# Attention and a tanh-shrink MLP: another order for the first batch's second layer, with weight rounding and weight combinations moved along with it

## The chip, the core and the metric

The kernel runs on one core of a Trainium2 chip. The core has a matrix engine (TensorE, "PE" in the profile, with its weight loads as "PEld"), a vector engine (VectorE, DVE), an activation engine (ScalarE, ACT), a general engine (GpSimd, POOL), and a queue engine (SyncE, SP) that issues the transfers between device memory and the core. Each engine works through its own list of instructions in order; an instruction that has to wait holds up everything behind it on that engine. The metric is the device time in microseconds (us) of one execution.

## What is computed

Attention over 8 batches and 12 heads, whose result is the input of a two-layer MLP:

```python
# q, k, v: (8, 12, 448, 64);  w_in: (768, 2048);  w_out: (2048, 768)
q_n = q / sqrt(mean(q * q) + 1e-6) * g_q          # k_n in the same way
attn = softmax(q_n @ k_n.T / sqrt(64)) @ v
x = attn.transpose(0, 2, 1, 3).reshape(8 * 448, 768)
h = x @ w_in
out = (h - tanh(h)) @ w_out
```

The weights are given in float64 and are rounded to float32 on the chip.

## The kernel before

The work goes in 48 attention steps (a step s is one batch and a pair of heads; six steps make a batch). Beside the attention of later steps runs the MLP of earlier batches, as a stream of matmuls that is cut into slices: `run(ns)` takes matmuls from the stream `mlp()` until their nominal time is used up, so that the order of all engines is fixed when the program is written. The MLP's matmuls are saved by a Strassen-like scheme: seven products (`ORDER` = 1, 5, 6, 2, 3, 7, 4) in place of eight, for which sums and differences of weight blocks and of activations are needed.

The first batch is special, because its weights are still being made ready. Its first layer (`hidden(0)`) is 28 products (4 groups j of 7), beside the steps 6 to 9. Its second layer (`project_first`, L1309) is plain: 6 chunks of 128 output columns, each the sum of 16 matmuls over the rows f of `w_out`, with 448 columns moving; 96 matmuls m in all, beside the steps 9 to 12. The chunks come one after another, each in its own PSUM bank (`mm_bank()`, three in turn): first the chunks 3 to 5, whose weights are the right half of `w_out` (`w_half[1]`), then 0 to 2 (`w_half[0]`). After the 16th matmul of a chunk ScalarE copies the bank out (L1345), VectorE transposes it (L966), and `step_out` later issues four transfers to the output.

The weights come in 32 pieces of 128 x 768 values (`PIECES`), 16 of `w_in` and 16 of `w_out` (pieces 16 to 23 the right half, 24 to 31 the left half, each holding two rows f). A piece n goes through these stages:

- SP loads it into a buffer `w_raw` (L290, L294), 768 KB. There are three buffers, and the load of piece n + 3 waits until piece n has left its own.
- `round_weight_a` on ScalarE (L71, L72), which waits for the load.
- `round_weight_b` on VectorE (L78, L79, L82); it is issued when the next piece takes the first stage.
- `round_weight_c` on POOL (L92 twice), after which the buffer is free.

How far `weight(to)` goes is a plan: `due` (L815) for the 28 products of the first layer, which end with 24 pieces done, and in the second layer the piece count 24 + 8 (m + 1) / 48 for its first 48 matmuls. For pieces of `w_in`, `combine` adds four combinations per group on VectorE (L357), one each product. Blocks that later batches need are written back to device memory (`keep_step` L372, `keep_w_out` and `keep_factors` L388).

For the second layer of later batches, `combine_w_out(f)` (L375) makes four combinations of `w_out` rows f and f + 8 on VectorE (L381 to L384, 128 x 384 each) into two slots of the ring `w_f` (six slots), and leaves behind two transfers to device memory, which are issued one round later. Before, this is done for f = 0 to 7 at the matmuls m = 52, 56, ... 80. The ring is then loaded for the next batch (`ring_load(2)` at m = 84 and `ring_load(4)` at 86).

The attention of a step s in this region (`early_slot`, L1448) emits, on PE: the sums over the keys (`totals`, L700) into a bank of the score pool, whose reciprocal VectorE takes (L705); the scores of the next step (L569), whose exponentials ScalarE takes (L575); a slice of 8 MLP matmuls; the transposes of the step after (`turn`, L467 and L471), the first of which goes to the bank that the reciprocal has just read; another 8 matmuls; then the remaining scores (with `p_last` for the last keys), the values (L623, L677), and `divide` on VectorE (L777, xT). The score pool has five banks that are taken in turn. From step 11 on, `visit` (L647) does this work, and takes `totals` of steps 11 and 12 to a bank of the MLP's pool.

Of the kernel before, what the change touches and what calls it, by code (L numbers as in the profile page):

```python
# [147 lines left out]
def bounded_path(tc, ctx, q, k, v, moe_w_in, moe_w_out, out, g_col, ident, ones, half_ones, neg_half, early):  # L148
# [29 lines left out]
    EARLY, PIECES = 8, 2 * CF  # L178
    HS = S // 2
    HC, HF = CD // 2, CF // 2  # L180
    SETS = CF // 4
# [83 lines left out]
    def w_out_row(f, i):  # L265
        return w_half[i][f // 2][:, f % 2]
# [35 lines left out]
    def weight_dst(n):  # L302
        return weight_piece(n)[2].rearrange("p f n -> p (f n)")
# [17 lines left out]
    def weight(to):  # L321

        while done[1] < min(to, PIECES):
            n = done[1]
            keep_step(0, {CF - 4: 0, CF: 1, CF + HF: SETS - 1}.get(n, -1))
            round_weight_a(nc, raws[n], weight_dst(n))
            settle(n)
            done[1] = n + 1
            load_weights(n + (3 if n < EARLY - 3 else 4))
            if kept[1] < kept[0] and n >= 4 * kept[0] + 2:  # L330
                keep_weights()
            keep_step(2)
        if done[1] == PIECES:
            settle(PIECES)
# [40 lines left out]
    def combine_w_out(f):  # L375

        a11, a21 = (w_out_row(f, i) for i in range(2))
        a12, a22 = (w_out_row(f + HF, i) for i in range(2))
        t = [ring_slot() for _ in range(2)]
        s3, s1, s2, s4 = (t[i // 2][:, i % 2 * HALF : (i % 2 + 1) * HALF] for i in range(4))  # L380
        nc.vector.tensor_tensor(out=s1, in0=a21, in1=a22, op=ALU.add)  # L381
        nc.vector.tensor_tensor(out=s3, in0=a11, in1=a21, op=ALU.subtract)
        nc.vector.tensor_tensor(out=s2, in0=s1, in1=a11, op=ALU.subtract)
        nc.vector.tensor_tensor(out=s4, in0=a12, in1=s2, op=ALU.subtract)  # L384
        late["keep"].append(lambda: [keep_factors(3 + 2 * i, 2, f, t[i]) for i in range(2)])

# [165 lines left out]
    def sc_bank():  # L552
        return bank_of("sc")
# [93 lines left out]
    def visit(s, av):  # L647

        wave(*half_values(s, 2, av, True))
        for c in range(2):  # L650
            v0, v1 = half_values(s, c, av, False)
            if has(s + 1):
                (s0, exp0), (s1, exp1) = scores(s + 1, c, True)
                wave(s0, v1)
                exp0()
                wave(v0, s1)
                exp1()
            else:
                wave(v0, v1)
        last_values(s, av)  # L660
        del loaded["v", s]
        if s >= FOLDED:
            divide(s, av)
        if has(s + 1):
            scores(s + 1, 2)
        if s < FOLDED:
            totals(s, mm_bank())
            divide(s, av)

    def values(s, av, chunks=(2, 0, 1)):  # L670
# [14 lines left out]
    def totals(s, dn):  # L685

        parts = [t[:, h, n * HS : (n + 1) * HS] for t in sums.get(s, ()) for n in range(2) for h in range(2)]
        parts = [(parts, [ones[:, :BL]] * 2)] if parts else []
        if not sums.pop(s):
            for p in full(s):  # L690
                parts.append(
                    ([p[:, h, n * HS : (n + 1) * HS] for n in range(2) for h in range(2)], [ones[:, :BL]] * 2)
                )
            last = probs[s, KF]
            parts.append(([last[:, h, 0] for _ in range(2) for h in range(2)], [half_ones[:, n] for n in range(2)]))
        for i, (moving, by) in enumerate(parts):
            for n in range(2):
                for h in range(2):
                    r = (2 * n + h) * BL
                    nc.tensor.matmul(  # L700
                        dn[r : r + BL, :HS], lhsT=by[n], rhs=moving[2 * n + h],
                        start=(i == 0), stop=(i == len(parts) - 1),
                    )
        rs = whole[s] = sp.tile([P, HS], F32, name="rs")
        nc.vector.reciprocal(rs, dn[:, :HS])  # L705
# [106 lines left out]
    late = {}  # L812


    due = [EARLY + (CF - EARLY) * (m + 1) // (7 * SETS // 2) for m in range(7 * SETS // 2)]  # L815
    due += [CF + HF * (m + 1) // (7 * SETS // 2) for m in range(7 * SETS // 2)]
    assert len(due) == 7 * SETS and due[-1] == CF + HF

    def part(name):
        if name == "th" and "blocks" in late:  # L820
            late["turn"] = (late.get("turn", 0) + 1) % 3
            if late["turn"] == 0:
                return late["blocks"].tile([P, 2, HS], F32, name="th_more")
        return tp.tile([P, 2, HS], F32, name=name)
# [484 lines left out]
    def project_first(b):  # L1309

        g = late["g"]
        for fn in late["todo"]:
            fn()
        late["todo"] = []
        keep_step(0, SETS - 1)
        took = 4 * S / ENGINE_NS
        for m in range(CD * CF):
            k, f = m // CF, m % CF
            n = (k + HC) % CD
            if f == 0:  # L1320
                bank = mm_bank()
            if f == CF // 2:
                step_out(2)
            if k < HC:
                weight(CF + HF + HF * (m + 1) // (HC * CF))
            elif m < HC * CF + 2:
                keep_w_out(PIECES - 2 + m - HC * CF)
            elif (m - HC * CF) % 4 == 0 and m - HC * CF <= 4 * HF:
                for fn in late["keep"]:
                    fn()  # L1330
                late["keep"] = []
                combine_w_out((m - HC * CF) // 4 - 1)
            elif m == CD * CF - 12:
                ring_load(2)
                for fn in late["keep"]:
                    fn()
            elif m == CD * CF - 10:
                ring_load(4)
            nc.tensor.matmul(  # L1339
                bank[:, :S], lhsT=w_out_row(f, n // HC)[:, n % HC * P : (n % HC + 1) * P], rhs=g[:, f, :],  # L1340
                start=(f == 0), stop=(f == CF - 1),
            )
            if f == CF - 1:
                y = part("s2").rearrange("p f s -> p (f s)")
                nc.scalar.copy(out=y, in_=bank[:, :S])  # L1345
                store(b, n, y)
            yield took
        wp_stack.close()
        late["blocks"] = pool("blocks", bufs=1)
        late["second"] = pool("second", bufs=1)  # L1350
        late["tg"] = single_stack.enter_context(tc.tile_pool(name="tg", bufs=1))
        late["inner"] = inner_steps()
# [527 lines left out]
```

## Time and profile before

| | us |
|---|---|
| median of 3 runs (1344.12 to 1344.48) | 1344.18 |
| the profiled execution | 1342.53 |
| its span, first to last instruction | 1340.7 |
| PE busy in the span | 1311.5 (98%) |
| VectorE busy | 969.5 (72%) |
| POOL busy | 795.0 (59%) |
| ScalarE busy | 568.1 (42%) |
| granted TensorE clock, mean | 0.998 |

The page's chain of waits gives 83% of the span to PE, 7% to VectorE and 4% to POOL. The regions that the change touches are the first layer of the first batch, whose matmuls (L857 on `w_out` and `w_f` buffers) run from 76.6 to 175 us, and its second layer (L1339), from 176.3 to 268.5. A timeline line has start, length, engine, source line, operation, output and inputs, shape and count; the bracket at the end is the idle time of the engine just before and who ended it. "PE <-DVE rs L705" there means that PE stood idle until VectorE's instruction of line 705 was done.

### The profile page before, as it was taken

Reading aid. Unit: us, or ns where it says so; the run is one execution under the profiler, and the core shown is the slowest. Engines: PE = TensorE matmul, PEld = TensorE weight load, DVE = VectorE, ACT = ScalarE, POOL = GpSimd, SP = SyncE. Lnnn points to the kernel's source line nnn. Section 1 sums busy time; section 2 is a strip of 40 time slices with the busy share of each in tenths; the row PEclk is TensorE's granted clock in tenths of the full one; section 3 lists DMA queues with packets and bytes.
Section 4 is the critical chain, followed back from the end, with each engine's and each line's share of the span. In section 5 each row is a group of like instructions: output and inputs, shape, how many; then the busy total and the mean of one; then the engine's idle time right before and its main releaser. Section 6 shows DMA issues by size and latency. Waiting matters only on the chain.

```text
span 1340.7 us, 29301 instructions
## 1 busy us (share of the span) xinstructions
PE 1311.5 (98%) x11368; PEld 1033.4 (77%) x11368; DVE 969.5 (72%) x1410; ACT 568.1 (42%) x1328; POOL 795.0 (59%) x591
## 2 busy tenths in 40 slices
PE   7989999999999999999999999999999999999997
PEld 3467854488998888688878788779887888799986
DVE  4999978867765767688888576768888667634455
ACT  7856654244343454445322445454512254311102
POOL 4766776348846256726698245944699244812771
PEclk9999999999999999999999999999999999999999
DMA  7779889889999766476655867466745776466544
GB/s 169 183 214 262 265 260 231 250 278 279 340 284 287 181 160 180 112 186 155 171 149 136 201 162 183 117 170 165 181 132 145 150 201 161 118 161 172 170 142 102
DMA packets 364759, 253.53 MB, mean 189 GB/s; under 512 B 273028, under 2 KB 303300, under 8 KB 364612
## 3 DMA queue, kind: packets, MB, share of 16 engines
q1 hardware_dynamic: 364608, 251.57, 69.1%
q8 instruction: 92, 1.51, 0.5%
q14 instruction: 55, 0.45, 0.1%
q10 hardware_dynamic: 4, 0.00, 0.0%
HBM read 205.23 MB, written 46.27 MB: 188 GB/s over the span
## 4 chain that ended last, share of the span: by engine, by line
PE 83%; DVE 7%; POOL 4%; DMA 2%; SPq 2%; issue 2%; ACT 1%; DVEq 0%; ACTq 0%; POOLq 0%
PE mm L857 38%; PE mm L1142 21%; PE sc L569 9%; PE sc L635 6%; PE mm L1339 5%; POOL u L1099 3%; PE sc L623 1%; POOL rr_mine L523 1%; PE sc L677 1%; DVE w_out L357 1%; PE mm L677 1%; SPq L497 1%; DVE rs L705 1%; DMA w_f<-w_inner 1%; DVE w_out L82 0%
## 5 line engine op out<-in xcount | busy, mean ns | idle before, releaser
L857 PE MATMUL mm<-xT,w_f 128*128 128x224 f32 x1296 | 263.5, 353 | 0.8 <-DVE xT L767 0.8
L857 PEld LDWEIGHTS mm<-xT,w_f 128*128 128x128 f32 x1296 | 244.8, 190 | 5.5 <-issue 4.2
L569 PE MATMUL sc<-qT,kT 64*32 64x448 f32 (+1 forms) x3072 | 215.6, 499 | 2.7 <-ACT p_last L575 2.1
L857 PE MATMUL mm<-tt,w_f 128*128 128x224 f32 x1044 | 212.6, 355 | 0.2 <-DMA w_f<-w_in 0.2
L857 PEld LDWEIGHTS mm<-tt,w_f 128*128 128x128 f32 x1044 | 195.8, 190 | 15.9 <-issue 15.4
L523 POOL TENSOR_TENSOR rr_mine<-rr_mine,neg_half 128x28 f32<-128x28 f32 x33 | 162.2, 4915 | 2.7
L762 DVE TENSOR_TENSOR xT<-xT,sc 128x448 f32<-128x448 f32 x34 | 21.0, 618 | 165.8 <-PE sc L569 114.8
L1142 PE MATMUL mm<-u,w_f 128*128 128x224 f32 x672 | 137.2, 354 | 1.0 <-POOL u L1099 0.5
L905 POOL TENSOR_TENSOR gT<-s,th 128x448 f32<-128x448 f32 x44 | 57.8, 1313 | 132.2 <-ACT th L904 128.7
L1142 PE MATMUL mm<-gT,w_f 128*128 128x224 f32 (+3 forms) x512 | 132.0, 412 | 1.2 <-DVE acc L1149 0.9
L1142 PEld LDWEIGHTS mm<-u,w_f 128*128 128x128 f32 x672 | 126.1, 190 | 8.0 <-POOL u L1099 3.6
L569 PEld LDWEIGHTS sc<-qT,kT 64*32 64x32 f32 x3072 | 72.4, 106 | 68.1 <-issue 49.2
L1142 PEld LDWEIGHTS mm<-gT,w_f 128*128 128x128 f32 x512 | 93.9, 190 | 34.3 <-issue 32.0
L635 PE MATMUL sc<-p,v_nat 64*32 64x448 f32 x1184 | 116.9, 536 | 0.0
L1142 PE MATMUL mm<-g,w_f 128*128 128x224 f32 (+1 forms) x360 | 98.9, 428 | 0.0
L575 ACT ACTIVATE p<-sc 128x448 f32<-128x448 f32 x132 | 71.9, 545 | 50.3 <-PE sc L569 37.4
L905 POOL TENSOR_TENSOR g<-s,th 128x448 f32<-128x448 f32 x24 | 30.3, 1264 | 105.1 <-ACT th L904 105.1
L1142 PEld LDWEIGHTS mm<-g,w_f 128*128 128x128 f32 x360 | 67.9, 190 | 26.5 <-issue 26.0
L729 ACT COPY sum_g<-sum 32x14 f32<-32x14 f32 x280 | 56.3, 201 | 72.0 <-DVE sum L721 66.3
L1339 PE MATMUL mm<-gT,w_out 128*128 128x448 f32 x192 | 74.0, 542 | 0.0
L145 POOL TENSOR_TENSOR rr<-rr,neg_half 112x8 f32<-112x8 f32 (+1 forms) x30 | 49.8, 1689 | 35.5 <-DVE rr L144 35.0
L1099 POOL TENSOR_TENSOR u<-gT 128x448 f32<-128x448 f32 x48 | 63.5, 1342 | 11.1 <-PE mm L1142 11.1
(206 smaller groups left out, 2465.8 us busy)
## 6 DMA issues: line engine op xcount, KB each, us to landing
w_f<-w_in SPq DMA_DIRECT2D x196, 384.0 KB, 3.5
w_f<-w_inner SPq DMA_DIRECT2D x63, 512.0 KB, 3.7
w_f<-w_out SPq DMA_DIRECT2D x42, 512.0 KB, 3.9
w_raw<-in_moe_w_out_dram SPq DMA_DIRECT2D x16, 768.0 KB, 5.4
w_in<-w_out SPq DMA_DIRECT2D x21, 384.0 KB, 5.3
qk_nat<-in_q_dram SPq DMA_DIRECT2D x132, 56.0 KB, 2.6
qk_nat<-in_k_dram SPq DMA_DIRECT2D x132, 56.0 KB, 2.4
g<-w_out SPq DMA_DIRECT2D x14, 512.0 KB, 5.4
```

Of the source, the lines that this page charges most:

```text
L145: nc.gpsimd.tensor_tensor(out=r, in0=r, in1=neg_half[:rows], op=ALU.pow)
L523: nc.gpsimd.tensor_tensor(out=mine, in0=mine, in1=neg_half[:, :1].to_broadcast([P, 2 * NJ]), op=ALU.pow)
L569: nc.tensor.matmul(tiles[h][i * BL : (i + 1) * BL, :n], lhsT=kT[r, c * P + at : c * P + at + BL], rhs=qT[r, first : first + n], start=True ...
L575: nc.scalar.activation(p[:, h, c if c < 2 else 0, :], tiles[h][:, :n], AF.Exp, scale=1.0 if rr is None else rr[:, 0, 2 * c + h : 2 * c + h ...
L635: nc.tensor.matmul(av[g][i * BL : (i + 1) * BL, :S], lhsT=v_nat[keys, h, c, m * BL : (m + 1) * BL], rhs=p[keys, h], start=first, stop=True ...
L677: nc.tensor.matmul(av[n][r : r + BL, :HS], lhsT=v_nat[:, h, c, m * BL : (m + 1) * BL], rhs=p[c][:, h, n * HS : (n + 1) * HS], start=False, ...
L729: nc.scalar.copy(out=acc[h * BL : (h + 1) * BL, g], in_=part[g * BL : (g + 1) * BL, h * NJ : (h + 1) * NJ])
L857: nc.tensor.matmul(bank[:, f * HS : (f + 1) * HS], lhsT=w[:, c * width + f, :], rhs=moving[p](c), start=(first and f == 0 and c == 0), sto ...
L905: eng.tensor_tensor(out=g[:, rows, cols], in0=h, in1=th, op=ALU.subtract)
L1099: nc.gpsimd.tensor_tensor(out=u[:, half], in0=a[:, half], in1=z[:, half], op=ALU.subtract)
L1142: nc.tensor.matmul(bank[:, :n], lhsT=w(i), rhs=mv, start=(first and i == 0), stop=(i == len(moving) - 1), skip_group_check=not first,)
L1339: nc.tensor.matmul(bank[:, :S], lhsT=w_out_row(f, n // HC)[:, n % HC * P : (n % HC + 1) * P], rhs=g[:, f, :], start=(f == 0), stop=(f == C ...
```

## The change

The first layer takes 14 pieces in its 28 products and ends with 22 done, where it took 16 and ended with 24; its plan starts two products later. The second layer then takes ten pieces in its first 44 matmuls (`behind`). To have time for the last two pieces of the right half, it works on three chunks at once: for each row f the three matmuls of three chunks, in three banks, twice. The copies and stores of three chunks then come together, at m = 45 to 47 and 93 to 95, into three different buffers. The combinations of `w_out` come at m = 24, 30, 36, ... 66. For the last two rows the four combinations leave in four transfers and not two. The ring loads come at m = 80 and 84. As the three MLP banks are all in use, `visit` takes `totals` of the steps 11 and 12 to the score pool.

```diff
-        late["keep"].append(lambda: [keep_factors(3 + 2 * i, 2, f, t[i]) for i in range(2)])
+        if f < HF - 2:
+            late["keep"].append(lambda: [keep_factors(3 + 2 * i, 2, f, t[i]) for i in range(2)])
+            return
+        late["keep"].append(lambda: [keep_factors(3 + n, 1, f, s) for n, s in enumerate((s3, s1, s2, s4))])
...
         if s < FOLDED:
-            totals(s, mm_bank())
+            totals(s, sc_bank())
...
-    due = [EARLY + (CF - EARLY) * (m + 1) // (7 * SETS // 2) for m in range(7 * SETS // 2)]
-    due += [CF + HF * (m + 1) // (7 * SETS // 2) for m in range(7 * SETS // 2)]
+    SOON_OUT, LAST_OUT = HF - 2, 44
+    due = [EARLY + (CF - EARLY + SOON_OUT) * max(m - 1, 0) // (7 * SETS - 2) for m in range(7 * SETS)]
+    behind = [min(PIECES, CF + SOON_OUT + (PIECES - CF - SOON_OUT) * (m + 1) // LAST_OUT) for m in range(CD * CF)]
...
         for m in range(CD * CF):
-            k, f = m // CF, m % CF
-            n = (k + HC) % CD
-            if f == 0:
-                bank = mm_bank()
-            if f == CF // 2:
-                step_out(2)
-            if k < HC:
-                weight(CF + HF + HF * (m + 1) // (HC * CF))
-            elif m < HC * CF + 2:
-                keep_w_out(PIECES - 2 + m - HC * CF)
-            elif (m - HC * CF) % 4 == 0 and m - HC * CF <= 4 * HF:
+            k, f, i = m // (HC * CF), m % (HC * CF) // HC, m % HC
+            n = (1 - k) * HC + i
+            if m % 4 == 3:
+                step_out()
+            weight(behind[m])
+            if f == 0:
+                bank = [] if i == 0 else bank
+                bank.append(mm_bank())
+            if LAST_OUT <= m < LAST_OUT + 2:
+                keep_w_out(PIECES - 2 + m - LAST_OUT)
+            if m >= CF + HF:
+                keep_combined((m - CF - HF) // 6 + 1)
...
-            elif m == CD * CF - 12:
+            if m == CD * CF - 16:
+                ring_load(2)
+            elif m == CD * CF - 12:
                 ring_load(4)
             nc.tensor.matmul(
-                bank[:, :S], lhsT=w_out_row(f, n // HC)[:, n % HC * P : (n % HC + 1) * P], rhs=g[:, f, :],
+                bank[i][:, :S], lhsT=w_out_row(f, n // HC)[:, n % HC * P : (n % HC + 1) * P], rhs=g[:, f, :],
                 start=(f == 0), stop=(f == CF - 1),
             )
             if f == CF - 1:
-                y = part("s2").rearrange("p f s -> p (f s)")
-                nc.scalar.copy(out=y, in_=bank[:, :S])
-                store(b, n, y)
+                y = part(("s2", "s5", "s1")[i]).rearrange("p f s -> p (f s)")
+                nc.scalar.copy(out=y, in_=bank[i][:, :S])
+                store(b, n, y, part("s2").rearrange("p f s -> p (f s)") if i == 2 else None)
```

`keep_combined(to)` issues the transfers that wait from the combination before, and then `combine_w_out(f)` for the rows up to `to`.

More of the change, by code (lines that the diff above doesn't have):

```diff
@@ L812, in bounded_path @@
     late = {}
-    due = [EARLY + (CF - EARLY) * (m + 1) // (7 * SETS // 2) for m in range(7 * SETS // 2)]
-    due += [CF + HF * (m + 1) // (7 * SETS // 2) for m in range(7 * SETS // 2)]
-    assert len(due) == 7 * SETS and due[-1] == CF + HF
+    SOON_OUT, LAST_OUT = HF - 2, 44
+    due = [EARLY + (CF - EARLY + SOON_OUT) * max(m - 1, 0) // (7 * SETS - 2) for m in range(7 * SETS)]
+    behind = [min(PIECES, CF + SOON_OUT + (PIECES - CF - SOON_OUT) * (m + 1) // LAST_OUT) for m in range(CD * CF)]
+    assert due[-1] == CF + SOON_OUT and due[7 * (SETS - 1) - 1] > CF
     def part(name):
@@ L1316, in project_first, with keep_combined @@
         took = 4 * S / ENGINE_NS
-        for m in range(CD * CF):
-            k, f = m // CF, m % CF
-            n = (k + HC) % CD
-            if f == 0:
-                bank = mm_bank()
-            if f == CF // 2:
-                step_out(2)
-            if k < HC:
-                weight(CF + HF + HF * (m + 1) // (HC * CF))
-            elif m < HC * CF + 2:
-                keep_w_out(PIECES - 2 + m - HC * CF)
-            elif (m - HC * CF) % 4 == 0 and m - HC * CF <= 4 * HF:
+        combined = [0]
+        def keep_combined(to):
+            for f in range(combined[0], min(to, HF)):
                 for fn in late["keep"]:
@@ L1331, in project_first @@
                 late["keep"] = []
-                combine_w_out((m - HC * CF) // 4 - 1)
-            elif m == CD * CF - 12:
-                ring_load(2)
+                combine_w_out(f)
+                combined[0] = f + 1
+        for m in range(CD * CF):
+            k, f, i = m // (HC * CF), m % (HC * CF) // HC, m % HC
[10 more added lines that the diff above has]
+                keep_combined((m - CF - HF) // 6 + 1)
+            if m == CF + HF + 6 * HF:
                 for fn in late["keep"]:
                     fn()
-            elif m == CD * CF - 10:
+                late["keep"] = []
+            if m == CD * CF - 16:
+                ring_load(2)
+            elif m == CD * CF - 12:
                 ring_load(4)
             nc.tensor.matmul(
-                bank[:, :S], lhsT=w_out_row(f, n // HC)[:, n % HC * P : (n % HC + 1) * P], rhs=g[:, f, :],
+                bank[i][:, :S], lhsT=w_out_row(f, n // HC)[:, n % HC * P : (n % HC + 1) * P], rhs=g[:, f, :],
                 start=(f == 0), stop=(f == CF - 1),
```

## The prediction

> **What bounds the kernel now.** First the page's slices and a table by stage, then the TensorE timeline for the idle gaps and who ends them, then VectorE, POOL, SP and ScalarE around the second layer.
>
> ```profile
> PE   7989999999999999999999999999999999999997
> 76.00:123.00 47.00, 40.11 (x332) 33.53 (x325) 45.03 (x61) 24.50 (x45) 29.43 (x22) 0.96 0.87 250
> 123.00:176.00 53.00, 53.00 (x518) 43.42 (x516) 49.63 (x69) 32.76 (x59) 38.50 (x29) 1.00 0.86 257
> 176.00:226.00 50.00, 50.00 (x354) 24.95 (x347) 40.16 (x47) 32.59 (x63) 33.07 (x29) 1.00 0.90 249
> ```
>
> The columns of the stages are length, then busy time of PE, weight load, VectorE, ScalarE and POOL. PE is full from 123 us on, through the whole second layer of the first batch (176 to 268). So nothing can be won there, and every new PE wait there adds to the end. Before 123, PE loses 6.9 us of 47, and VectorE is busy for 45.
>
> ```profile
> 83.77 0.66 PE L467 MATMUL sc<-ident,qk_nat 128*128 128x128 f32 x4 [1.57 <-DVE rs L705]
> 91.15 2.81 PE L857 MATMUL mm<-xT,w_out 128*128 128x224 f32 x8 [2.54 <-DVE s L926]
> 120.70 0.66 PE L467 MATMUL sc<-ident,qk_nat 128*128 128x128 f32 x4 [2.32 <-DVE rs L705]
> ```
>
> These are PE's gaps (in brackets) in that stage. All three wait for VectorE, which stands behind its own queue. They are the whole prize.
>
> ```profile
> 192.40 1.65 DVE L777 TENSOR_TENSOR xT<-sc,rs 64x224 f32<-64x224 f32 x4 [1.20 <-PE sc L677]
> 194.08 0.56 DVE L78 TENSOR_SCALAR w_out<-w_out 128x768 f32<-128x768 f32 x1
> ...
> 208.67 0.95 DVE L966 STREAM_TRANSPOSE th<-s 128x448 f32<-128x448 f32 x1
> 209.65 1.56 DVE L705 RECIPROCAL rs<-sc 128x224 f32<-128x224 f32 x1
> 211.12 0.50 DVE L78 TENSOR_SCALAR w_out<-w_out 128x768 f32<-128x768 f32 x1
> ```
> ```profile
> 214.07 0.60 PE L467 MATMUL sc<-ident,qk_nat 128*128 128x128 f32 x4
> 224.34 0.98 PE L569 MATMUL sc<-qT,kT 64*32 64x448 f32 x16
> ```
> ```profile
> 213.65 2.42 POOL L92 TENSOR_TENSOR w_out<-w_out,w_raw 128x384 int32<-128x384 int32 x2 [2.45 <-ACT w_out L71]
> 216.09 0.37 SPq L294 DMA_DIRECT2D w_raw<-in_moe_w_out_dram  x1
> 221.52 0.95 ACT L71 ACTIVATE w_out<-w_raw 128x768 f32<-128x768 f32 x1 [3.07 <-DMA w_raw<-in_moe_w_out_dram]
> 223.22 0.51 ACT L1345 COPY s<-mm 128x448 f32<-128x448 f32 x1
> 223.63 0.78 ACT L575 ACTIVATE p_last<-sc,rr 128x224 f32<-128x224 f32 x2
> ```
>
> The reader is to see two thin covers. First: from the xT multiply at 192.40, which waits for PE, VectorE has no gap until past 211, and the reciprocal it ends with (done 211.2) must free the bank that PE's transposes take at 214.07: cover 2.9 us. Second: POOL's adds for piece 28 end at 216.07, SP loads piece 31 at 216.09 into the room they free, ScalarE waits 3.07 us for it, and the exponential behind it is done at about 224.08 (half of the pair at 223.63), while PE wants its bank at 224.34: cover 0.3 us.
>
> **What the Trainium skill says.** "SBUF — State Buffer", section "Who interferes with whom": a VectorE instruction in a two-port mode, or with two SBUF inputs while GpSimd reads SBUF, and a GpSimd instruction exclude each other. The trace agrees: L79 takes 0.56 us in some passes and 1.25 in others, and a pass of L78, L79 and L82 took 2.06 to 3.79 us. "TensorE: Matmul & The Clock Gate", section "HAM oscillation — how this bites in real kernels": PE gaps over some 3.4 us bring back the slow clock. Here the 2.54 us gap already did: the 12 instructions after it took 2.73 us and not 2.28, with 0.6 more in the next group, some 1.05 in all; the 2.32 us gap cost nothing visible. "DMA: Bandwidth & Descriptors", section "Latency and other measured facts": some 2 us of a transfer are fixed. Here a 768 KB piece takes 5.4 us from issue to landing, and that is used.
>
> **The change, part by part.** A piece passes ScalarE (L71, L72, 1.7 us), VectorE (a pass), POOL (L92 twice, 2.0 to 3.7), each in program order.
>
> *Fewer pieces beside the first layer.* By the order of instructions the reciprocal of step 7 (at 119.09) has two passes and three L357 adds fewer before it: 2 x 2.8 + 3 x 1.2, so it is 9 us earlier or simply on time after PE's sums (end 111.15), and the 2.32 us gap goes. The gaps at 83.77 and 91.15 stay: the same VectorE instructions stand ahead of L705 and L926 there. The first-layer weights have slack: pieces 8 to 11 and 12 to 15 are due some four products (9 us and more) before their use. Gain 2.32; what is late next is nothing up to 176.
>
> *Three chunks at once.* The same 96 matmuls on three banks. I take 0: instructions of 224 columns come every 191.5 ns (16.09 us for 84 in the chain of waits), those of 448 every 382 (12.22 for 32), so there is no fixed part that another order of banks could save, and none that it could add without a cause; -0.5 to +0.5. The pieces are due some 30 matmuls before their rows are multiplied, so PE does not wait for weights. But the three copies out of the banks now come together behind piece 31 on ScalarE: two more than before, 2 x 0.41 = 0.82 us, ahead of the exponentials. The transposes of the store (L966, 0.98 with its gap) leave matmuls 15 and 31.
>
> *Ten pieces and early combinations.* Between the xT multiply at 192.40 and the reciprocal VectorE now has four passes and not three, two combinations of four adds, and no transpose. A pass is 2.79 on the mean of the ten at 174 to 225 (2.06 to 3.79); a combination 2.30 on the mean of eight at 230 to 260 (1.97 to 3.28). So 2 x 2.30 + 2.79 - 0.98 = 6.4 us (5.0 to 9.4). VectorE cannot start sooner, since xT waits for PE; its 6 us of gaps before 192 are of no use for what is queued behind it. First wait: the reciprocal ends at 211.2 + 6.4 = 217.6, PE's transposes of L467 want it at 214.07: 3.5 us, and all matmuls, the next scores and values queue behind it. Second: piece 28's pass comes 6.4 later, so do POOL's adds, the load of piece 31, its landing and its ScalarE part, then 0.82 for the copies. Behind ScalarE's wait stand the copies and the exponentials p_last and p_full of step 11. The one that frees PE's bank is done at 224.08 + 7.2 = 231.3 against 224.34: 7.0 us. This contains the first wait, it doesn't add to it (5.6 to 9.9 by the bounds). Each combination also has two SP transfers: 1.1 us of issue, in a wait of SP for POOL's adds; cost 0, up to 1 if SP gets late with piece 31.
>
> *The rest.* Later VectorE has about two combinations fewer to do per step and catches up; sums for step 11 are ready some 4 us before PE. The totals of two steps go to a score bank whose exponential is 0.3 us older: 0 to 0.3 each. The last two combinations go out in eight transfers and not four, 4 x 0.5 us on SP before the ring loads; these came at 258 to 263 with PE needing them at 274.5, so some 5 us are left: 0. The slow clock after the new gaps: 0 to 1, I take 0.3.
>
> Sum: -2.3 + 7.0 + 0.3 = +5.0 us (3.3 to 8). The profiled execution took 1342.53 (span 1340.7), so it would be 1347.5; the median shown is 1.65 above that execution, so 1344.18 + 5.0 = 1349.2.
>
> **Rivals.**
> *Only the bank wait counts*: if the load of piece 31 comes no later than PE's own 3.5 us of delay hides, because pieces flow more evenly, the sum is 3.5 - 2.3 = +1.2: 1345.4. For it: VectorE's passes 22 and 23 come early. Against: rooms for raw pieces come free one by one, at 201, 206, 211 and 216 in the trace, each load within 0.1 us of POOL's end.
> *The relief reaches back* (faster): without the later passes VectorE and POOL collide less from 83 on, and the gaps at 83.77 and 91.15 and the slow clock go too. That is the idle time of the stage, 6.9, and its slow clock, 0.04 of 47 = 1.9, against the loss at its low price, 5.6: -8.8 + 5.6 = -3.2, 1341.0. It decides if L926 at product 1 comes 2.5 us sooner. For it: the pass at 86.16 took 3.5 us and not 2.1. Against: the instructions ahead of it are the same.
> *Dearer*: piece 24 is loaded only after POOL's last tanh product (184.5 to 185.6), lands near 194 and holds the exponentials of step 10, which PE wants at 192.6; with slower clock on top, +9 or more: 1353 and above.
>
> **How the numbers follow.** Forecast 0.68 (own range 1347.5 to 1352.2, from +3.3 and +8 with the slow clock), dearer 0.07, only the bank wait or nothing at all 0.11, relief 0.14. A measurement of this kernel tells no change from 0.2%, 2.7 us. Slower by more: 0.75; within: 0.11; faster: 0.14. The range, 1340.8 to 1353.5, takes in the small case and the middle of the fast one, and leaves out half of the fast case and most of the dearer one: about 0.15 in all.
>
> **What would show it.** Right: no PE gap near 118 us; PE waiting some 3 to 4 us for a reciprocal at the transposes before matmul 40; a ScalarE wait for the load of piece 31 with three copies and p_last behind it, and PE waiting there or at matmul 48. Wrong: those passes and combinations at the low prices throughout, the gap at 91 gone, or PE without a gap from 176 to 226.

## The result, and the profile after

The changed kernel takes 1353.16 us (median of 6 runs, 1349.01 to 1354.75), the kernel before 1344.15 in runs on the same chip: a ratio of 1.0061, 95% interval 1.0043 to 1.0079. It is slower by about 9 us. Its profiled execution took 1350.45 us (span 1348.6), against 1342.53 (span 1340.7) before: 7.9 us between the two. In the profiles this difference splits as follows, each length read from the TensorE rows of the timeline (start of the first-layer matmuls near 77 us, start of the first and end of the last matmul of the second layer). The two rows of before that bound its second layer:

```profile
176.25 6.28 PE L1339 MATMUL mm<-gT,w_out 128*128 128x448 f32 x16
...
250.36 18.22 PE L1339 MATMUL mm<-gT,w_out 128*128 128x448 f32 x48
```

| us | before | after | difference |
|---|---|---|---|
| up to the first-layer matmuls near 77 | 76.66 | 77.26 | +0.6 |
| from there to the second layer | 99.59 | 94.49 | -5.1 |
| second layer of the first batch, with the attention in it | 92.33 | 103.95 | +11.6 |
| from there to the end of the span | 1072.1 | 1072.9 | +0.8 |

So in the profiles the change wins in the first layer and loses more than twice that in the second. The page's slices of the changed kernel and the table by stage (columns as before) show where:

```profile
PE   7989997999999999999999999999999999999997
```
```profile
76.00:123.00 47.00, 42.44 (x367) 36.36 (x346) 43.45 (x62) 26.86 (x50) 27.37 (x22) 1.00 0.77 224
123.00:176.00 53.00, 53.00 (x511) 41.83 (x510) 50.33 (x66) 35.87 (x68) 39.86 (x31) 1.00 0.87 270
176.00:226.00 50.00, 44.38 (x274) 22.25 (x276) 46.16 (x55) 23.72 (x40) 30.50 (x25) 0.93 0.86 231
226.00:280.00 54.00, 51.68 (x411) 25.04 (x409) 38.36 (x58) 16.13 (x30) 18.44 (x16) 1.00 0.80 219
```

In the slices a 7 stands in the seventh place, where TensorE was full before. In the table TensorE was busy for 50.00 of 50 us from 176 to 226; now it is 44.38, at a clock of 0.93, while VectorE rose from 40.16 to 46.16. The TensorE timeline of the changed kernel (start, length, tile, count, idle time before and who ended it):

```profile
84.37 0.66 PE L470 MATMUL sc<-ident,qk_nat 128*128 128x128 f32 x4 [1.57 <-DVE rs L708]
91.76 1.78 PE L861 MATMUL mm<-xT,w_out 128*128 128x224 f32 x8 [2.54 <-DVE s L930]
...
117.21 0.60 PE L470 MATMUL sc<-ident,qk_nat 128*128 128x128 f32 x4
...
171.75 6.28 PE L1352 MATMUL mm<-gT,w_out 128*128 128x448 f32 x16
...
215.57 1.11 PE L470 MATMUL sc<-ident,qk_nat 128*128 128x128 f32 x4 [5.62 <-DVE rs L708]
...
217.22 7.73 PE L1352 MATMUL mm<-gT,w_out 128*128 128x448 f32 x16
...
231.47 0.98 PE L572 MATMUL sc<-qT,kT 64*32 64x448 f32 x14 [2.32 <-ACT p_last L578]
232.38 12.29 PE L1352 MATMUL mm<-gT,w_out 128*128 128x448 f32 x32
```

The gap of 2.32 us that stood at 120.70 is gone; those of 1.57 and 2.54 stayed. Two new ones stand in the second layer: 5.62 us for the reciprocal and 2.32 us for the exponential p_last. Between them 16 matmuls take 7.73 us and not 6.19: this is the slow clock, granted at half from 213.49 to 220.32 us. VectorE ahead of the first new gap:

```profile
187.90 1.65 DVE L780 TENSOR_TENSOR xT<-sc,rs 64x224 f32<-64x224 f32 x4 [2.52 <-PE sc L680]
...
200.50 1.25 DVE L381 TENSOR_TENSOR w_f<-w_out,w_out 128x384 f32<-128x384 f32 x1
...
209.53 0.57 DVE L381 TENSOR_TENSOR w_f<-w_out,w_out 128x384 f32<-128x384 f32 x1
210.02 1.34 DVE L382 TENSOR_TENSOR w_f<-w_out,w_out 128x384 f32<-128x384 f32 x1
211.29 1.36 DVE L383 TENSOR_TENSOR w_f<-w_f,w_out 128x384 f32<-128x384 f32 x1
212.75 1.18 DVE L384 TENSOR_TENSOR w_f<-w_out,w_f 128x384 f32<-128x384 f32 x1
213.96 1.56 DVE L708 RECIPROCAL rs<-sc 128x224 f32<-128x224 f32 x1
```

From the xT multiply to the reciprocal VectorE has no gap, and takes 213.96 - 187.90 = 26.06 us where it took 209.65 - 192.40 = 17.25. And the way of piece 31, in the timelines of POOL, SP and ScalarE:

```profile
207.49 3.63 POOL L145 TENSOR_TENSOR rr<-rr,neg_half 112x8 f32<-112x8 f32 x2
211.09 2.42 POOL L92 TENSOR_TENSOR w_out<-w_out,w_raw 128x384 int32<-128x384 int32 x2
217.65 2.49 POOL L92 TENSOR_TENSOR w_out<-w_out,w_raw 128x384 int32<-128x384 int32 x2 [4.14 <-issue]
...
215.12 3.94 SPq L117 DMA_DIRECT2D v_nat<-in_v_dram  x2
219.10 1.25 SPq L127 DMA_DIRECT2D v_nat<-in_v_dram  x2
220.40 1.79 SPq L391 DMA_DIRECT2D w_out<-w_out  x2
222.35 0.40 SPq L294 DMA_DIRECT2D w_raw<-in_moe_w_out_dram  x1
...
228.08 0.92 ACT L71 ACTIVATE w_out<-w_raw 128x768 f32<-128x768 f32 x1 [5.23 <-DMA w_raw<-in_moe_w_out_dram]
229.70 1.37 ACT L1358 COPY s<-mm 128x448 f32<-128x448 f32 x3
230.96 0.80 ACT L578 ACTIVATE p_last<-sc,rr 128x224 f32<-128x224 f32 x2
```

POOL's adds for piece 28 end at 220.14, the load of piece 31 goes out at 222.35, ScalarE waits 5.23 us for it, and behind it stand the three copies and p_last. That load goes out 222.35 - 171.75 = 50.6 us after the start of the second layer; before it was 216.09 - 176.25 = 39.84. The difference, 10.8 us, is nearly the whole growth of the layer, 11.6.

### The profile page after: what moved, and what is told of

It reads as the page before. It is cut to its first block, busy times and chain, and to the rows that moved or that the text cites. A ratio compares the mean times of both kernels' runs of the same rounds, so it can differ in the third digit from the quotient of the medians.

```text
span 1348.6 us, 29309 instructions
## 1 busy us (share of the span) xinstructions
PE 1313.0 (97%) x11368; PEld 1034.3 (77%) x11368; DVE 973.1 (72%) x1410; ACT 568.3 (42%) x1328; POOL 793.0 (59%) x591
## 4 chain that ended last, share of the span: by engine, by line
PE 80%; DVE 7%; POOL 5%; DMA 2%; issue 2%; SPq 2%; ACT 1%; ACTq 0%; DVEq 0%; POOLq 0%
PE mm L861 38%; PE mm L1146 21%; PE sc L572 8%; PE sc L638 6%; PE mm L1352 4%; POOL u L1103 2%; POOL rr_mine L526 1%; PE sc L626 1%; DMA w_f<-w_in 1%; PE sc L680 1%; DVE w_out L82 1%; DVE rows L616 1%; DVE w_out L357 1%; DVE w_out L79 0%; DVE rs L708 0%
## 5 line engine op out<-in xcount | busy, mean ns | idle before, releaser
L92 POOL TENSOR_TENSOR w_out<-w_out,w_raw 128x384 int32<-128x384 int32 x40 | 48.2, 1226 | 38.8 <-issue 11.5
```

The lines of the kernel that those rows point to most:

```text
L92: nc.gpsimd.tensor_tensor(out=bits[:, part], in0=bits[:, part], in1=raw[:, part, 0], op=ALU.add)
```

## The experiments

The ten kernels of the experiments ran in three groups, each group on one chip together with the kernel before; the ratio is to the runs of before in the same group, whose medians were 1342.72 to 1343.20 us. So ratios can be compared, and medians of different groups only to about 1.5 us. The rows of before and of the change repeat the result above. The last three columns are worked out from one profile of each kernel as in the table above: first layer (from the matmuls near 77 us to the second layer), second layer, and the time from the start of the second layer to the load of piece 31.

| kernel | median us | ratio, 95% interval | first layer | second layer | load 31 |
|---|---|---|---|---|---|
| before | 1344.15 | 1 | 99.59 | 92.33 | 39.84 |
| the change | 1353.16 | 1.0061, 1.0043 to 1.0079 | 94.49 | 103.95 | 50.60 |
| chunks_only | 1342.93 | 1.0003, 0.9994 to 1.0011 | 99.21 | 92.33 | 39.74 |
| early_comb_only | 1352.30 | 1.0072, 1.0058 to 1.0086 | 100.06 | 99.39 | 46.85 |
| comb_from_36 | 1345.13 | 1.0013, 1.0005 to 1.0022 | 100.32 | 92.33 | 40.09 |
| late_comb | 1346.94 | 1.0031, 1.0019 to 1.0044 | 96.10 | 99.62 | 44.86 |
| late_comb_rooms | 1339.63 | 0.9966, 0.9953 to 0.9980 | 94.49 | 92.77 | 33.74 |
| piece31_gp | 1349.66 | 1.0054, 1.0036 to 1.0072 | 96.10 | 102.88 | 48.67 |
| late_comb_60 | 1343.45 | 1.0001, 0.9992 to 1.0010 | 94.49 | 92.39 | 50.00 |
| late_comb_60_ring | 1344.36 | 1.0006, 0.9997 to 1.0015 | 96.10 | 92.38 | 50.00 |
| cand1 | 1341.93 | 0.9991, 0.9982 to 1.0000 | 96.08 | 96.60 | 52.40 |
| rooms_comb44 | 1340.80 | 0.9983, 0.9974 to 0.9991 | 94.15 | 93.87 | 33.75 |

**The three chunks alone.** The kernel before with the new order of matmuls, on three banks:

```diff
-            k, f = m // CF, m % CF
-            n = (k + HC) % CD
+            k, f, i = m // (HC * CF), m % (HC * CF) // HC, m % HC
+            n = (1 - k) * HC + i
...
-            totals(s, mm_bank())
+            totals(s, sc_bank())
```

> The kernel before with one thing of the change: three chunks at once on three banks (totals of the folded steps on a score bank, as that needs), pieces, combinations and due times as before. Theory (VectorE's queue): the order of the matmuls costs nothing, two copies more stand before the exponentials: 0 to +1 us, 1343.5 to 1345.5. Rival A (order, banks or copies cost): +4 us and more, 1348 and above. Rival B: no change.

1342.93 us, and the second layer lasts 92.33 us to the hundredth as before. The order, the banks and the totals on a score bank cost nothing. Two of the copies stand ahead of piece 31 on ScalarE here and the third behind it, so three copies behind piece 31, as in the change, are not tested by this run.

**The early combinations alone.**

```diff
-            elif (m - HC * CF) % 4 == 0 and m - HC * CF <= 4 * HF:
...
+            if m >= CF + HF and (m - CF - HF) % 6 == 0 and m <= CF + HF + 6 * HF:
                 for fn in late["keep"]:
                     fn()
...
-                combine_w_out((m - HC * CF) // 4 - 1)
...
+                if m < CF + HF + 6 * HF:
+                    combine_w_out((m - CF - HF) // 6)
```

> The kernel before with one thing of the change: the combinations of w_out at matmuls 24, 30, ... 66 (pieces, chunk order and due times as before, ring loads at 84 and 86). Theory (VectorE's queue): two combinations, 4.6 to 7.2 us, stand ahead of the reciprocal that has 2.9 us of cover, and ahead of the last pieces that have 0.3: TensorE waits 2 to 4 us at the transposes and up to 4.3 to 6.9 us in all, so 1348 to 1351 us. Rivals A and B (chunk order or piece plan cost): within 2 us of before, 1343 to 1346.

1352.30 us: one part of the change gives a loss as large as the whole change, somewhat more than I expected of it (1351 at most). VectorE, POOL and SP in its timeline, with the two TensorE rows that wait:

```profile
206.53 1.26 DVE L381 TENSOR_TENSOR w_f<-w_out,w_out 128x384 f32<-128x384 f32 x1
...
212.96 0.55 DVE L381 TENSOR_TENSOR w_f<-w_out,w_out 128x384 f32<-128x384 f32 x1
213.42 2.48 DVE L382 TENSOR_TENSOR w_f<-w_out,w_out 128x384 f32<-128x384 f32 x1
...
217.94 1.56 DVE L705 RECIPROCAL rs<-sc 128x224 f32<-128x224 f32 x1
...
221.94 2.66 POOL L92 TENSOR_TENSOR w_out<-w_out,w_raw 128x384 int32<-128x384 int32 x2 [6.46 <-ACT n L132]
...
224.63 0.37 SPq L294 DMA_DIRECT2D w_raw<-in_moe_w_out_dram  x1
...
219.56 0.66 PE L467 MATMUL sc<-ident,qk_nat 128*128 128x128 f32 x4 [3.79 <-DVE rs L705]
232.93 0.98 PE L569 MATMUL sc<-qT,kT 64*32 64x448 f32 x14 [0.42 <-ACT p_last L575]
```

The two combinations take 2.8 us (206.53 to 209.30) and 4.0 us (212.96 to 216.95), 6.8 together. Here SP sends the load within 0.03 us of POOL's end (224.60). It is 46.85 - 39.84 = 7.0 us late, and the layer grows by 7.1: the lateness of this one load is the loss of the layer. The wait at the transposes and what follows it lie inside. The profile is 9.6 us longer than that of before; the other 2.5 us lie before the layer (1.5) and after it (1.0), where the combinations do not stand, and their cause was not looked for.

**A smaller dose.** The same with the combinations at matmuls 36, 40, ... 64, behind the reciprocal.

```diff
-            if m >= CF + HF and (m - CF - HF) % 6 == 0 and m <= CF + HF + 6 * HF:
+            if m >= 36 and (m - 36) % 4 == 0 and m <= 36 + 4 * HF:
...
-                    combine_w_out((m - CF - HF) // 6)
+                    combine_w_out((m - 36) // 4)
```

> The kernel before with one thing of the change in a smaller dose: the combinations of w_out at matmuls 36, 40, ... 64, so that none stands ahead of the reciprocal (before matmul 40) or of the pass for piece 28, while all come far earlier than before. Theory (what costs is the two combinations that stand ahead of the reciprocal and of piece 28, 6.8 us of VectorE's queue in the run with early combinations alone): no wait at the transposes, the load of piece 31 within 1 us of its old place against the start of the second layer (39.8 us after it), 1342 to 1344.5 us. Rival (early combinations cost wherever they stand, by collisions with GpSimd's adds and by their transfers on SyncE): 1347 and above.

1345.13 us, somewhat over what I expected, but the second layer is back at 92.33 us, with the load at 40.09. In this timeline the reciprocal, and the first combination behind it:

```profile
209.96 1.56 DVE L705 RECIPROCAL rs<-sc 128x224 f32<-128x224 f32 x1
...
213.44 0.55 DVE L381 TENSOR_TENSOR w_f<-w_out,w_out 128x384 f32<-128x384 f32 x1
```

The reciprocal starts 33.4 us into the layer, as before. So it is not combining early that costs, it is standing ahead of the reciprocal and of the pass for piece 28. Where the remaining 1.9 us of the median come from is not settled; the profile has 2.7 us more after the second layer, with only small TensorE waits in it.

**The change without its early combinations.** Combinations at 52 to 80 again, ring loads at 84 and 86; three chunks and ten pieces in 44 matmuls stay.

```diff
-            if m >= CF + HF:
-                keep_combined((m - CF - HF) // 6 + 1)
-            if m == CF + HF + 6 * HF:
+            if m >= HC * CF + 4:
+                keep_combined((m - HC * CF - 4) // 4 + 1)
+            if m == CD * CF - 12:
...
```

> The changed kernel with the eight combinations of w_out at their old places (matmuls 52 to 80, their transfers with them, ring loads at 84 and 86); the three chunks and the ten pieces in 44 matmuls stay. Theory (VectorE's queue ahead of the reciprocal and of piece 28 holds the loss, and most of that queue is the two early combinations, 2.8 and 4.4 us in the profile): the reciprocal comes some 7 us earlier against TensorE, so the 5.6 us wait at the transposes goes; the exponentials behind piece 31 are late by 1 to 3 us at most (one pass more and two copies more than before). The first layer keeps its gain of about 5, so 1340 to 1343 us, below the kernel before. Rival A (the three chunks, their copies or their banks cost): nothing changes at the scores, the time stays above 1350. Rival B (the ten pieces in 44 matmuls cost): at most half of the loss goes, 1346 to 1350, with the wait at the reciprocal still over 3 us.

1346.94 us: a miss, this is still slower than before. The time lies in the range of rival B, but the wait at the reciprocal that it named is gone; the other wait stayed:

```profile
212.30 0.60 PE L474 MATMUL sc<-ident,n 112*128 112x112 f32 x4 [1.19 <-ACT p L578]
226.38 0.98 PE L572 MATMUL sc<-qT,kT 64*32 64x448 f32 x14 [3.17 <-ACT p_last L578]
...
213.77 2.30 POOL L92 TENSOR_TENSOR w_out<-w_out,w_raw 128x384 int32<-128x384 int32 x2 [1.54 <-ACT p L578]
...
212.73 2.19 SPq L117 DMA_DIRECT2D v_nat<-in_v_dram  x2
...
217.55 0.41 SPq L294 DMA_DIRECT2D w_raw<-in_moe_w_out_dram  x1
```

The load of piece 31 is at 44.86, 5.0 us late: POOL's adds for piece 28 end 3.6 us later into the layer (216.07 - 172.69 = 43.4, before 39.8), and SP comes to the load 1.5 us after that, behind the loads of v and two transfers. The copies make it 5.6 by the start of matmul 48 (227.29 - 172.69 = 54.60, before 49.01). After the 3.17 us gap the next 32 matmuls take 13.99 us and not 12.29. I had counted one VectorE pass for the two additional pieces and had taken the rest of their way as free.

**More room for the pieces.** To late_comb two rooms are added: pieces 28 and 29 land in a part of the ring that is free until matmul 56. Piece 31 then takes the room of piece 26.

```diff
+    EXTRA = (28, 29)
...
-            raw = wp.tile([P, 2 * DM], I32, name="w_raw", bufs=3)
+            raw = wp.tile([P, 2 * DM], I32, name="w_raw", bufs=3) if n not in EXTRA else ring[
+                :, 2 * SLOT + EXTRA.index(n) * 2 * DM : 2 * SLOT + (EXTRA.index(n) + 1) * 2 * DM
+            ].bitcast(I32)
...
-        return n - 3 < max(done[2], EARLY)
+        return n in EXTRA or n - (5 if EXTRA[1] < n < EXTRA[1] + 4 else 3) < max(done[2], EARLY)
...
-            load_weights(n + (3 if n < EARLY - 3 else 4))
+            load_weights(n + (3 if n < EARLY - 3 else 4 if n < EXTRA[0] - 4 else 6))
```

> The changed kernel with late combinations (matmuls 52 to 80) as in the run of that name, and with two more rooms for raw pieces: pieces 28 and 29 land in the part of the ring that is free until matmul 56, so that piece 31 takes the room of piece 26 and no longer waits for GpSimd's adds of piece 28. Theory (the loss behind the ten pieces is the load of piece 31 that waits for a room, 5.0 us later than before against the start of the layer, with its copies): the 3.2 us wait at the scores and the 1.2 us before it go or fall under 1 us in all, the second layer lasts 92.5 to 94 us and not 99.6. The ring loads of the next batch may then be late, as with the pieces over 60 matmuls, so the time is 1339 to 1344. Rival (ten passes cost on VectorE, whatever the rooms): the second layer still lasts over 97 us, 1346 and above.

1339.63 us, faster than both kernels. SP and ScalarE in its timeline:

```profile
205.79 0.37 SPq L296 DMA_DIRECT2D w_raw<-in_moe_w_out_dram  x1
...
217.00 1.06 ACT L71 ACTIVATE w_out<-w_raw 128x768 f32<-128x768 f32 x1
...
218.77 1.41 ACT L1360 COPY s<-mm 128x448 f32<-128x448 f32 x3
220.03 0.84 ACT L581 ACTIVATE p_last<-sc,rr 128x224 f32<-128x224 f32 x2
```

The load is out 33.74 us into the layer, ScalarE no longer waits for it, and TensorE has no gap there: 92.77 us, 0.44 more than before. The same ten passes run on VectorE as in late_comb, and from 176 to 226 us VectorE is busy for 46.32 us, as long as in the change (46.16). So neither the number of pieces nor VectorE's load costs more than this 0.44 by itself. What costs is that the last load waits for a room which VectorE and POOL free late.

**SP's share.** The change with the load of piece 31 issued by GpSimd, right behind the adds that free its room.

```diff
-            nc.sync.dma_start(
+            (nc.gpsimd if n == PIECES - 1 else nc.sync).dma_start(
                 out=raw.rearrange("p (f c) -> p f c", f=2),
```

> The changed kernel with one edit: the load of piece 31 is issued from GpSimd's queue, right behind the adds of piece 28 that free its room, and not from SyncE's, where it stands behind the loads of v and the transfers of two combinations. Theory (of the 11.6 us that the second layer grew, 2.2 are SyncE's queue between the end of those adds and the load): the load comes within 1 us of the adds' end, the wait at the reciprocal stays (5 to 6 us), the one at the scores behind the exponentials falls from 3.2 us to about 1; the second layer lasts 101 to 102.5 us and not 104, the time is 1350 to 1352. Rival (SyncE's place costs nothing, since memory or GpSimd's own issue is as late): no change, 1352 to 1354.

1349.66 us; the interval overlaps with that of the change. The timeline shows a part of what I expected:

```profile
218.59 2.49 POOL L92 TENSOR_TENSOR w_out<-w_out,w_raw 128x384 int32<-128x384 int32 x2 [4.14 <-issue]
221.39 0.91 POOL L294 DMA_DIRECT2D w_raw<-in_moe_w_out_dram  x1 [0.30 <-POOL w_out L92]
...
216.52 1.12 PE L470 MATMUL sc<-ident,qk_nat 128*128 128x128 f32 x4 [5.30 <-DVE rs L708]
231.36 0.98 PE L572 MATMUL sc<-qT,kT 64*32 64x448 f32 x14 [1.32 <-ACT p_last L578]
```

The load is 0.31 us behind the adds and not 2.21, the wait at the scores falls from 2.32 to 1.32, and the layer by 1.1 us. The landing takes longer by this way (221.39 to ScalarE's start at 227.92, 6.5 us, against 5.7), which takes back most of the rest. The gain is read from one profile of each kernel; the runs do not tell the two kernels' times apart.

**Pieces over 60 matmuls, and further versions.** late_comb with the ten pieces spread, so that the last two stand behind the exponentials of step 11 on ScalarE:

```diff
-    SOON_OUT, LAST_OUT = HF - 2, 44
+    SOON_OUT, LAST_OUT = HF - 2, 60
```

> The changed kernel with the combinations at their old places (matmuls 52 to 80) and the ten pieces spread over 60 matmuls instead of 44, so that the last two pieces come after the exponentials of step 11 on ScalarE. Theory (VectorE's queue, then one late transfer in ScalarE's order): both waits of the second layer go, nothing is late there, and the first layer keeps its gain of about 5: 1338 to 1340.5 us. Rival A (three chunks cost): above 1347. Rival B (ten pieces cost however they are spread, by VectorE passes and collisions): 1343 to 1346.

1343.45 us: a miss in the sum, although the second layer is as short as expected (92.39). This run shows the second half of the mechanism. Its load of piece 31 goes out at 50.00 us, nearly as late as in the change (50.60), and ScalarE waits for it, but the exponential now stands ahead of that wait and not behind it:

```profile
217.60 0.77 ACT L578 ACTIVATE p_last<-sc,rr 128x224 f32<-128x224 f32 x2
...
225.39 0.91 ACT L71 ACTIVATE w_out<-w_raw 128x768 f32<-128x768 f32 x1 [2.66 <-DMA w_raw<-in_moe_w_out_dram]
```

Here, then, the late load costs the layer nothing, since no exponential that TensorE is about to need stands behind it on ScalarE. But TensorE now reaches the second batch earlier than its blocks; the timeline of TensorE and SP:

```profile
287.25 3.18 PE L861 MATMUL mm<-tt,w_f 128*128 128x224 f32 x8 [3.71 <-DMA w_f<-w_in]
...
281.63 2.04 SPq L500 DMA_DIRECT2D qk_nat<-in_k_dram  x4
283.77 1.84 SPq L430 DMA_DIRECT2D w_f<-w_in  x4
```

I took SP's order for the cause and put one block's load ahead of the loads for the attention:

```diff
-                ring_load(ring_steps.index((b, layer, j, p)) + 5)
+                step = ring_steps.index((b, layer, j, p))
+                ring_load(step + (6 if step == 1 else 5))
```

> The run with ten pieces over 60 matmuls and late combinations, with one more edit: in the second batch's second product the ring is filled one block further ahead, so that this block's load stands on SyncE ahead of the eight loads for the attention and not behind them. Theory (the 5 us won in the first layer were lost again because SyncE's queue, full of the twelve stores of the three chunks, was late with that block: a wait of 3.7 us and the slow clock after it): most of it comes back, 1338.5 to 1341 us, no wait over 1.5 us there. Rival (something else is late at the same place, the block after it or the memory's bandwidth): 1342.5 to 1344.

1344.36 us: no gain, as the rival said. In the profile, of the slowest of its 14 executions (1348.46), TensorE waits elsewhere (2.54 us at 290.90 for a VectorE operation of the attention, 2.41 at 435.96 for a block). What holds these versions back after the second layer stays open. Two more versions put combinations close behind the pieces. cand1 has the pieces over 60, that ring edit, and combinations at 40, 45, ... 75:

```diff
-            if m >= CF + HF:
-                keep_combined((m - CF - HF) // 6 + 1)
-            if m == CF + HF + 6 * HF:
+            if m >= 40:
+                keep_combined((m - 40) // 5 + 1)
+            if m == 79:
```

> The changed kernel with three edits: the ten pieces over 60 matmuls, the combinations at matmuls 40, 45, ... 75 (ring loads at 80 and 84 as in the change), and the ring block of the second batch's second product filled one further ahead. Theory: none of the waits of the second layer, ring loads earlier than with late combinations, first layer's gain of about 5 kept: 1338 to 1340.5 us. Rival (combinations between the pieces cost by collisions): 1343 and above, with waits at the scores behind the exponentials.

1341.93 us, between theory and rival. TensorE waits 2.23 us at 249.08 for n, the attention's norms on VectorE, which now stand among pieces and combinations; that these delay them is read from the order and was not tested. rooms_comb44 is late_comb_rooms with combinations at 44, 48, ... 72 and ring loads at 80 and 84:

```diff
-            if m >= HC * CF + 4:
-                keep_combined((m - HC * CF - 4) // 4 + 1)
-            if m == CD * CF - 12:
+            if m >= 44:
+                keep_combined((m - 44) // 4 + 1)
+            if m == CD * CF - 16:
...
```

> The run with two more rooms for raw pieces, with the combinations at matmuls 44, 48, ... 72 instead of 52 to 80 and the ring loads at 80 and 84 as in the change: all of them stand behind the reciprocal and the load of piece 31. Theory: the second layer lasts 92.3 to 93.5 us as with late combinations, the next batch's blocks are there earlier: 1338 to 1340.5 us. Rival (combinations close behind the pieces delay VectorE's norms for the scores after matmul 64, as in the run with combinations from matmul 40): a wait of 1 to 3 us at the transposes there, 1341 to 1344.

1340.80 us, with a wait of 0.50 us at 239.26 and a layer of 93.87 us: between theory and rival, and no better than late_comb_rooms (ratio 0.9983 and not 0.9966).

## Why the prediction was right in direction and low in size

It said slower, for the reason that the runs confirm. The forecast of 1349.2 is 4.0 us under the measured median, which lies above the forecast's own range of 1347.5 to 1352.2 and only 0.3 us inside the stated one (its top is 1353.5). That it lies inside is in part luck, since two terms of the sum were too small and their errors cancel in part.

- **First layer, -2.3.** The gap at 120.70 went and the two others stayed, as written. The stage gained 5.1 us in the profiles. Like for like it is 3.5: with the new due times it lasts 96.1 us where the slow clock followed the gap of 2.54 (four profiles) and 94.2 to 94.5 where it did not (four); before had it, with 99.59. With the old due times all four profiles have the slow clock somewhere in this layer: in early_comb_only and comb_from_36 not at 91 but at the gap near 120 (2.61 us there), and the layer lasted 100.06 and 100.32. So the gap that went also took along a place where the slow clock can come, which the prediction put at nothing. Besides the gap some 1 us came from attention groups that ran stretched before. The prediction also misread the slow clock of before: the row at 91.15 has 8 instructions, not 12. Up to the next group they took 2.73 us, where the change without the slow clock took 1.71 (91.76 to 93.47), and some 1.6 us were lost in all, not 1.05. That gap stayed, so this did not enter the sum.
- **Three chunks, 0.** Right: 92.33 us with and without. The copies, +0.82, were 1.37 - 0.51 = 0.86.
- **VectorE ahead of the reciprocal, +6.4 (5.0 to 9.4).** It was 26.06 - 17.25 = 8.8. The step that failed is the price of the combinations: the first took 2.8 us, the second 4.4, not 2.30 each, and the second also more than the 3.28 that I had as the bound of one. The mean came from combinations at 230 to 260, where POOL has less to do (in before 12.84 us of 24 from 226 on, 0.56 of 15 from 250 on, against 33.07 of 50 from 176 to 226). The second stands beside POOL's work (L145 until 211.12, then the adds of L92 until 213.51, in the profile after), and three of its four adds took 1.2 to 1.4 us where 0.55 is the short value. The twelve profiles agree: of the 384 adds of combinations, the 196 with no POOL instruction beside them all took 0.52 to 0.56 us, and the 106 that took over 0.7 all had one (82 had one and stayed short). This fits the exclusion that the Trainium skill's "SBUF — State Buffer" describes in "Who interferes with whom"; I had cited it, with the spread of the passes beside it, and then priced the combinations without it. The first wait was 5.6 us and not 3.5.
- **SP, 0 (up to 1).** It cost 2.2 us between POOL's end and the load in the profile after, behind the loads of v (3.94 us for two) and two transfers; moving that load to another queue gave half of it back in the layer.
- **The second wait contains the first.** Right, and it settles the sum: counted from the start of the layer, matmul 48 starts at 60.63 and not 49.01. The 11.6 us are 8.8 from VectorE, less 0.2 at POOL, 2.2 from SP, 0.3 in landing and 0.9 in copies, less the cover of some 0.3. The forecast had 7.0.
- **Slow clock, 0.3 on top.** It came and slowed the matmuls after the 5.62 us gap (7.73 us for 16 and not 6.19), but it lies inside the wait for piece 31 and adds nothing here. In late_comb, where it follows the last wait, it does cost 1.7.
- **Ring loads, totals: 0.** No wait for the ring shows in the profile after. The 0.8 us more behind the second layer are in part small waits (TensorE idle for 3.6 us there and not 3.1); the rest was not traced.
- **The rivals.** "Only the bank wait" fell: the load of piece 31 is later, not hidden. "The relief reaches back" fell: the gap at 91 is as long as before. "Dearer" gave about the right time for a wrong reason: the scores of step 10 lost 0.2 us, not several.

The two errors have opposite signs: 2.8 too little gain in the first layer, 4.6 too little loss in the second. With 1.4 us outside the two layers and less the 0.3 for the slow clock, they make 2.9 of the 4.0 us. The other 1.1 are between profile and median: the median of the changed kernel lies 2.7 above its profiled execution, that of before 1.6.

That the parts do not add up is part of the reading. Early combinations alone cost 7.1 us of the second layer and the ten pieces without them 7.3 (5.6 without the slow clock), together 11.6. Both act through the one load: it goes out 7.0 us late with the one, 5.0 with the other and 10.8 with both. And the slow clock of late_comb comes after the last wait, that of the change inside it, where it costs nothing more. Where the remaining 1.2 us between 7.0 + 5.0 and 10.8 go was not worked out.

## What to carry to other kernels

Find the last thing in the chain (here one load that needs a room, with exponentials behind it in the same queue) and count every operation that a change puts ahead of it on each queue it passes, priced where it will stand and not where it stood. Work taken from a busy stage is a gain only if the next stage has cover, and here a buffer made it: two more rooms turned +0.31% (the change with late combinations) into -0.34%. When a stall is removed, look at what TensorE then reaches too early.

## What the runs showed of the hardware that was not expected

The same gap of 2.54 us at 91 us was followed by the slow clock in six of twelve profiles and not in the other six: the 8 matmuls after it took 2.63 to 3.15 us, or 1.78. It is worth 1.6 us in the length of the stage (96.1 against 94.5). The Trainium skill, "TensorE: Matmul & The Clock Gate", "HAM oscillation — how this bites in real kernels", speaks of gaps over some 3.4 us; here shorter ones did it, down to 2.15 us (late_comb_rooms, at 342.05).

The clock records of the twelve traces show an order in this. From 24 us to 15 us before the end of the span, every slow stretch is half clock for 3.41 us or twice that, and within a profile all of them begin on one grid of 3.413 us: in chunks_only at 67.37, 91.27 and 121.98, which is 7 and 9 steps apart. Cut along this grid, the profiles have 19 steps in which TensorE was idle for 55% or more, and the clock was halved after each of them. After steps with less idle time it was halved once (45%, in chunks_only at 67.37). So the gap of 2.54 us was followed by the slow clock where it fell into one step (74% of it idle, in before), and not where it was split over two (41% and 34%, in the change). Where the grid lies differs from profile to profile.

A single profile can by this alone differ from another of the same kernel by 1.6 us. The changed kernel's profile was one without the slow clock at 91, which may be a part of the 2.7 us between its 1350.45 and the median of 1353.16.

The load of piece 31 (768 KB) issued by GpSimd took 6.5 us from issue to use, and the one issued by SyncE 5.7, in kernels that differ only in this. Where ScalarE waits for that load in other profiles, SyncE's took from 4.8 (late_comb_60) to 6.0 us (cand1), so that one load by GpSimd is thin evidence.
